# Causal attention and a PReLU MLP on one Trainium2 core: last outputs stored by half, first K loads on ACT's queue, four roundings of x moved to ACT, residues of sums of x spread over more steps

## The chip, the cores and the metric

The kernel runs on one core of a Trainium2 chip. The metric is the device time of one execution in microseconds (us), taken as the median of several executions. Five engines run their own instruction streams and wait for one another by semaphores: PE (TensorE, matrix products), DVE (VectorE), ACT (ScalarE), POOL (GpSimd) and SP (SyncE, which here only issues DMAs). DMAs go through queues that an engine's stream feeds; here nearly all are issued by SP.

## The reference

```python
scores = scale * q @ k.T            # per batch (4) and head (12): 448 x 448, D = 64
scores = where(causal mask, -1e9, scores) - max
attn = exp(scores); attn = attn / (sum(attn) + 1e-9)
a = attn @ v                         # (4, 12, 448, 64), fp32
x = a.transpose(0, 2, 1, 3).reshape(1792, 768)
h = x @ w_in                         # 768 -> 2048
g = max(h, 0) + alpha * min(h, 0)    # PReLU, alpha per column
out = g @ w_out                      # 2048 -> 768, fp32
```

## The kernel before

**Attention.** The 12 heads of a batch are 6 pairs of heads, so there are 24 pairs p in all; TURNS gives their order, batches 0 and 1 first (p 0 to 11), then 2 and 3 (p 12 to 23). They run as a software pipeline: iteration n of the loop in `attention` goes once through the list ORDER, and an entry such as `EX30+2` does step EX30 of pair p = n - 2. For one pair the steps are: load q and k (LQ, LK), scores on PE into PSUM (S0 to S2, SF), row maximum on DVE (MX, line 429), exponential with row sum on ACT (EX, line 444), reciprocals of the seven columns of row sums at once on DVE (RC, `row_rec`), scaling of the rows on POOL, or on DVE for a few (NO), transposes on PE (PT, line 472), their copies out of PSUM on ACT or DVE (C), and the product with v (AV, line 491). All engines but SP go through the same list, so the list sets the order of each engine's stream. AV has lag 4: iteration n does AV of pair n - 4.

**What AV leaves.** The result x of a pair (128x448 in PSUM) is rounded to fp32r as x_hi (XH on ACT for the parts named B, XN on DVE for those named N, which are the pairs 10, 11, 14, 15, 22, 23 by `part_of`), its rest x_lo is computed on DVE (XL, line 553) and stored to a DRAM scratch. The MLP's first product uses a Strassen-like scheme for all groups but the first, so sums T1 to T4 of parts of x are kept in fp32 in `spare` (XF, DVE), and each of the 16 sums must be rounded (`t_hi`) and its residue taken and stored (`t_lo`). In EARLY these are marked `T` (both on POOL); in FIRST they are `th` (rounding on ACT) and `tl` (residue on DVE, then its store when the next one is taken).

**The weights** arrive as 8-byte doubles and are decoded per piece of 128x384: abs on ACT (line 243), clamp on POOL (246), four operations on DVE (249 to 257), add on POOL (260). Then casts to fp32r on ACT (lines 287, 317) and the low parts on POOL (291, 320). The table EARLY says in which iteration of the attention which of these are done for the first group: `A` abs, `C` clamp, `D:i:k` k of the DVE operations of piece i, `+` add, `LD` load of the next piece, `cast:` and `sub:` the two halves of a split. LOADV says how many of the loads of v are issued in the iteration in which AV of pair p is done.

**The MLP.** The 2048 columns are 8 groups g of 256, each for two blocks of tokens bp; together 16 units q = 2g + bp. A unit has four result tiles X, Y, Z, W of h in PSUM; `h_act` applies PReLU on DVE, `g_hi` (line 731, ACT) and `g_lo` (line 735, POOL) split it, and `o_half` (line 769, PE) multiplies a 128-row tile with one half (384 columns) of w_out and adds it to `acc` (line 775 on ACT for group 0, line 777 on DVE after that). For the last group the finished rows go to the output (line 785, SP). Behind the attention, group 0 is written out by hand: FIRST lists for the steps 0 to 28 what the engines do beside PE; steps 1 to 10 have one `h_mms` of unit 1 each on PE, the later ones one or two `o_half`. Entries are `act.1X` (PReLU of unit 1's X), `gh`, `gl`, `D`, `abs`, `clamp`, `add`, `S` (a sum of weight pieces), `cast`, `sub`, `th`, `tl`.

**DMA counters.** The hardware queue's transfers report to eight counters in turn, shared by all engines that issue; an issue waits until the transfer that used its counter before, eight earlier in the program, has landed.

Of the kernel before, what the change touches and what calls it, by code (L numbers as in the profile page):

```python
# [10 lines left out]
F32 = mybir.dt.float32  # L11
# [5 lines left out]
ALU = mybir.AluOpType  # L17
# [16 lines left out]
LOADV = {0: 2, 1: 2, 2: 2, 3: 1, 9: 4, 10: 3, 12: 1, 13: 2, 14: 2, 15: 2}  # L34
TURNS = [(0, 0), (0, 1), (0, 2), (0, 5), (1, 0), (1, 1), (1, 3), (1, 4), (0, 3), (0, 4), (1, 2), (1, 5)]
ORDER = """
E2+4 LK+0 LQ+0 LT+4 NO00+3p NO10+3p MX11+2 NO21+3p NO11+3p EX10+2 EX11+2 MX20+2 NO20+3p MX21+2 EX20+2 NO30+3p MX00+2 EX00+2 AV+4 S2+2 LV+4 PT1+3 PT0+3 PT2+3 EX21+2 MX01+2 EX01+2 XF+4 XN+4 XH+4 C10+3a MX30+2 XL+4 EX30+2 ED+4 C00+3d C21+3d RC+2 NO01+2p C20+3a PT3+3 S0+1 S1+1 SF+1 C30+3a EA+4 MX10+1 ST+4
# [9 lines left out]
7: gl.1Y clamp.i2.1 S.S1.1 th
8: D.i2.1.2 tl cast.S1.1
9: D.i2.1.2 load sub.S1.1 abs.i3.1 cast.L1.1
10: add.i2.1 clamp.i3.1 sub.L1.1 th  # L50
11: act.1W act.1Z tl
12: D.i3.1.2 S.S2.1 cast.A22.1
13: D.i3.1.2 load sub.A22.1 th
14: add.i3.1 S.S3.1 cast.A11.1 tl
# [63 lines left out]
def kernel(  # L118
# [455 lines left out]
    def run(it, n=None):  # L574
# [4 lines left out]
        "LV": load_v_next, "RC": row_rec, "AV": av, "XH": x_hi, "XN": x_hi_plain, "XF": x_sums, "XL": x_lo, "ST": lambda p: flush(stores),  # L579
# [8 lines left out]
    for nm in "qk":  # L588
        steps["L" + nm.upper()] = lambda p, nm=nm: p and load(p, nm)
# [168 lines left out]
    def o_half(q, n, t, hf):  # L758
# [318 lines left out]
```

## Time and profile before

| quantity | value |
|---|---|
| time, 3 runs | 627.35, 628.26 (median), 629.2 us |
| the profiled execution's own time | 627.45 us |
| its span, first to last instruction | 625.7 us |
| PE busy | 608.4 us, 97% of the span, 3528 matmuls |
| DVE / ACT / POOL busy | 501.7 (80%) / 277.2 (44%) / 395.7 us (63%) |
| HBM read / written | 105.00 / 14.68 MB, 191 GB/s over the span |

The span covers the first to the last instruction; the execution's own time is 1.75 us longer than that. "Busy" counts computing instructions only. PE is busy nearly everywhere, so what is left is in the few places where PE has nothing to do: at the start, at stalls during the attention and just behind it, and at the end, where the last outputs are still under way. A stall of another engine costs only where PE ends up waiting for it.

### The profile page before, as it was taken

The page shows a single profiled execution, that of the slowest core. Times are in us where ns is not written, and L with a number is a line of the kernel's source. Part 1 is how long each engine was busy: PE and PEld are TensorE (multiplying, and loading weights), DVE is VectorE, ACT ScalarE, POOL GpSimd, SP SyncE. Part 2 cuts the span into 40 slices and gives each one's busy share as a digit, 9 for nine tenths or more (in the row PEclk, how much of TensorE's full clock was granted, in tenths as well). Part 3 has the DMA queues.
Part 4 walks back from the last instruction along what each step waited for, and adds up shares of the span by engine and source line. Part 5 has one row for each costly group of instructions (what it writes and reads, how often), then busy time and mean ns, then how long its engine had stood idle before and what let it go on. Part 6 is the DMA issues. An engine that isn't in the chain of part 4 may idle for free.

```text
span 625.7 us, 10851 instructions
## 1 busy us (share of the span) xinstructions
PE 608.4 (97%) x3528; PEld 529.6 (85%) x3528; DVE 501.7 (80%) x1117; ACT 277.2 (44%) x766; POOL 395.7 (63%) x530
## 2 busy tenths in 40 slices
PE   7899999999999899999999999999999999999996
PEld 3566676666878799899999999989999999999896
DVE  5699999999688579798689879868977987895363
ACT  5789897898344655231333323232332323232110
POOL 4455676868776758865775687567667766763120
PEclk9899999999999999999999999999999999999999
DMA  5874477642868468656765775786667567554535
GB/s 130 194 184 135 117 223 208 204 134 70 281 188 287 136 207 288 212 181 204 246 190 176 230 215 155 222 250 177 191 221 221 179 218 224 166 175 140 178 137 201
DMA packets 87736, 120.39 MB, mean 192 GB/s; under 512 B 12032, under 2 KB 64256, under 8 KB 87680
## 3 DMA queue, kind: packets, MB, share of 16 engines
q1 hardware_dynamic: 87520, 119.48, 62.6%
q8 instruction: 28, 0.46, 0.3%
q10 hardware_dynamic: 160, 0.23, 0.1%
q14 instruction: 28, 0.23, 0.1%
HBM read 105.00 MB, written 14.68 MB: 191 GB/s over the span
## 4 chain that ended last, share of the span: by engine, by line
PE 82%; DVE 6%; DMA 4%; SPq 3%; POOL 2%; ACT 1%; issue 1%; POOLq 0%; ACTq 0%; DVEq 0%
PE o L769 35%; PE heldY L676 11%; PE heldX L676 8%; PE heldZ L676 5%; PE pt L472 5%; PE a L491 4%; PE s L417 3%; PE h_V L676 3%; PE heldW L676 2%; DMA v<-in_v_dram 2%; PE s L409 2%; SPq L352 2%; ACT p L444 1%; SPq L355 1%; DVE s L429 1%
## 5 line engine op out<-in xcount | busy, mean ns | idle before, releaser
L777 DVE TENSOR_TENSOR acc<-o,acc 128x384 f32<-128x384 f32 x196 | 107.5, 552 | 71.2 <-PE o L769 70.9
L398 POOL TENSOR_SCALAR p<-p,rs 128x128 f32<-128x128 f32 (+3 forms) x164 | 80.4, 512 | 57.2 <-DVE rs L453 34.4
L444 ACT ACTIVATE p<-s,nm 128x256 f32<-128x256 f32 (+3 forms) x168 | 82.0, 497 | 20.1 <-DVE nm L429 19.8
L769 PE MATMUL o<-wo,g_X 128*128 128x384 f32 x336 | 76.8, 335 | 2.9 <-ACT g_X L731 1.8
L769 PE MATMUL o<-wo,g_Z 128*128 128x384 f32 x336 | 76.6, 335 | 1.1 <-DVE t_W L722 0.6
L429 DVE CUSTOM_DVE_ANT_0 s<-s,mask 128x256 f32<-128x256 f32 (+3 forms) x168 | 70.9, 480 | 8.0 <-PE s L417 5.7
L769 PE MATMUL o<-wo,g_W 128*128 128x384 f32 x336 | 76.6, 334 | 0.3 <-POOL g_W L735 0.3
L769 PE MATMUL o<-wo,g_Y 128*128 128x384 f32 x336 | 76.4, 335 | 0.0
L769 PEld LDWEIGHTS o<-wo,g_X 128*128 128x128 f32 x336 | 60.3, 188 | 6.7 <-ACT g_X L731 2.1
L769 PEld LDWEIGHTS o<-wo,g_Z 128*128 128x128 f32 x336 | 60.2, 188 | 4.9 <-DVE t_W L722 0.9
L769 PEld LDWEIGHTS o<-wo,g_W 128*128 128x128 f32 x336 | 59.9, 188 | 0.6 <-POOL g_W L735 0.6
L769 PEld LDWEIGHTS o<-wo,g_Y 128*128 128x128 f32 x336 | 60.0, 188 | 0.0
L491 PEld LDWEIGHTS a<-ptf,v 128*64 128x64 f32 x384 | 27.7, 136 | 35.1 <-issue 10.5
L472 PEld LDWEIGHTS pt<-ident,p 128*128 128x128 f32 x384 | 44.6, 144 | 13.7 <-issue 10.9
L491 PE MATMUL a<-ptf,v 128*64 128x64 f32 (+3 forms) x384 | 49.5, 387 | 3.6 <-DMA v<-in_v_dram 2.3
L472 PE MATMUL pt<-ident,p 128*128 128x128 f32 x384 | 48.7, 279 | 2.4 <-DVE p L460 1.3
L260 POOL TENSOR_TENSOR y_i<-y_i,x_i 128x384 f32<-128x384 f32 x32 | 33.5, 1048 | 27.1 <-DVE x_i L257 27.1
L260 POOL TENSOR_TENSOR y_o<-y_o,x_o 128x384 f32<-128x384 f32 x32 | 32.4, 1012 | 15.9 <-DVE x_o L257 15.9
L394 ACT ACTIVATE ptf<-pt 128x512 f32<-128x512 f32 (+1 forms) x72 | 38.3, 574 | 8.6 <-PE pt L472 8.6
L735 POOL TENSOR_TENSOR g_Z<-t_Z,g_Z 128x384 fp32r<-128x384 f32 (+1 forms) x16 | 20.0, 1247 | 31.1 <-ACT g_Z L731 31.1
L417 PE MATMUL s<-kr,qr 64*128 64x128 f32 (+2 forms) x288 | 38.4, 394 | 0.0
L243 ACT ACTIVATE x_i<-raw_i 128x384 f32<-128x384 f32 x32 | 17.8, 555 | 46.3 <-DMA raw_i<-in_moe_w_in_dram 46.3
(177 smaller groups left out, 1339.4 us busy)
## 6 DMA issues: line engine op xcount, KB each, us to landing
lo_T<-low_T SPq DMA_DIRECT2D x28, 512.0 KB, 4.6
lo_B<-low_B SPq DMA_DIRECT2D x25, 512.0 KB, 4.7
raw_i<-in_moe_w_in_dram SPq DMA_DIRECT2D x32, 384.0 KB, 3.8
raw_o<-in_moe_w_out_dram SPq DMA_DIRECT2D x32, 384.0 KB, 3.3
lo_T<-low_T SPq DMA_DIRECT2D x28, 384.0 KB, 3.9
lo_B<-low_B SPq DMA_DIRECT2D x25, 384.0 KB, 3.9
lo_N<-low_N SPq DMA_DIRECT2D x16, 512.0 KB, 4.8
lo_N<-low_N SPq DMA_DIRECT2D x16, 384.0 KB, 4.5
```

The costliest lines, as they stand in the source:

```text
L260: nc.gpsimd.tensor_tensor(out=y, in0=y, in1=xf, op=ALU.add)
L394: eng.activation(out, x, AF.Copy, scale=side)
L398: eng.tensor_scalar(out=out, in0=x, scalar1=side, scalar2=1.0, op0=ALU.mult, op1=ALU.mult)
L417: nc.tensor.matmul(ps[:, o : o + lim], T["q", p][half(j), i * QP : (i + 1) * QP], T["k", p][half(j), :lim], start=(o == 0), stop=(n > 0 or ...
L429: nc.vector.tensor_tensor_reduce(out=t, in0=t, in1=masks[1] if i == NQ else masks[0][:, (NQ - 1 - i) * QP :], scale=-SCALE, scalar=MOST_F3 ...
L444: nc.scalar.activation(T["p", p, i][:, j, : t.shape[1]], t, AF.Exp, scale=-1.0, bias=T.pop(("nm", p, i, j)), accum_out=T["sm", p][:, z : z ...
L472: nc.tensor.transpose(ps[:, j - js[0], c], t[:, j, c * QP : (c + 1) * QP], T["ident"])
L491: nc.tensor.matmul(out[half(j), c * QP :], vs[b % 2][:, hp, c, j], x[:, c * QP : S], start=(c == 0), stop=(c == NQ),)
L676: nc.tensor.matmul(ps, w[:, u, k * P : (k + 1) * P], x, start=(first and i == 0), stop=(i == len(mms) - 1), skip_group_check=True,)
L735: nc.gpsimd.tensor_tensor(out=l, in0=hts.pop((q, nm)), in1=h, op=ALU.subtract)
L769: nc.tensor.matmul(ps[:, :NH], x, w, start=(i == 0), stop=(i == 3 * GC - 1))
L777: nc.vector.tensor_tensor(out=a[:, cols], in0=ps[:, :NH], in1=a[:, cols], op=ALU.add)
```

## The change

1. **Outputs.** Each 128x384 half of the last group is stored as soon as it is added; before, both halves of a tile were stored together behind the second half, the very last tile apart. The output bytes are the same; SP issues 24 more DMAs.
2. **First K.** The K of pairs 0, 1 and 2 (six DMAs of 64x448) are issued by ACT at its start; before, only pair 0's were, and those of pairs 1 and 2 came from SP.
3. **RA.** For pair 0 alone the seven reciprocals are taken in two steps: six columns in a new step RA behind EX01, the seventh in RC as before. In the list ORDER, `RA+2` stands between `EX01+2` and `XF+4`, so ahead of `MX30+2`.
4. **ROUND.** x_hi of the pairs 10, 11, 14, 15 is rounded by ACT (XH), not DVE (XN).
5. **EARLY and LOADV.** The decoding of the first group's weights and the sums T are given to other iterations (before: DVE operations in iterations 12 to 19 numbered 2, 2, 2, 2, 2, 1, 1, 1; now 1, 1, 3, 3, 1, 0, 3, 1), and v of batches 2 and 3 is loaded in 2, 3, 2 DMAs with pairs 12 to 14, not 1, 2, 2, 2 with 12 to 15.
6. **FIRST.** The residues (`th`, `tl`) run from step 2 to 24, not 2 to 16; `gh.1X`, `gl.1X` stand at step 16, one step earlier, and `1W` at 17, with the casts S2 and S3 one step later.

```diff
-    5: "A:0", 6: "C:0 D:0:1", 7: "D:0:2 A:1", 8: "C:1", 12: "D:0:1 LD D:1:1 T",
-    13: "+:0 D:1:2 A:2 cast:A21", 14: "C:2 D:1:1 LD D:2:1 +:1", 15: "D:2:2 A:3 T",
-    16: "C:3 sub:A21 D:2:1 LD D:3:1 cast:A22", 17: "D:3:1 T", 18: "+:2 D:3:1 sub:A22 cast:L1", 19: "D:3:1 LD T",
-    20: "+:3 cast:A11", 21: "sub:L1 cast:A12", 22: "sub:A11 cast:L0 A:4", 23: "sub:A12 C:4 A:5", 24: "sub:L0 C:5",
-    25: "LD +:4 T D:5:4 LD", 26: "C:6 C:7 D:6:4 LD T T +:6 T T",
+    5: "A:0", 6: "C:0 D:0:1", 7: "D:0:2 A:1", 8: "C:1", 12: "D:0:1 LD T", 13: "+:0 D:1:1 A:2 cast:A21",
+    14: "C:2 D:1:3 LD", 15: "D:2:3 +:1", 16: "D:2:1 LD T A:3 cast:A22", 17: "+:2 C:3 cast:L1 cast:A11",
+    18: "D:3:3 T", 19: "D:3:1 LD +:3 sub:A21", 20: "T sub:A22 cast:A12", 21: "sub:L1 sub:A11 cast:L0",
+    22: "sub:A12 sub:L0 A:4", 23: "C:4 A:5", 24: "C:5", 25: "LD +:4 T D:5:4 LD", 26: "C:6 C:7 D:6:4 LD T T +:6 T T",
 }
 FRONT = {25: "D:4:4", 26: "+:5 A:6 A:7"}
...
-LOADV = {0: 2, 1: 2, 2: 2, 3: 1, 9: 4, 10: 3, 12: 1, 13: 2, 14: 2, 15: 2}
+LOADV = {0: 2, 1: 2, 2: 2, 3: 1, 9: 4, 10: 3, 12: 2, 13: 3, 14: 2}
+ROUND = (10, 11, 14, 15)
 TURNS = [(0, 0), (0, 1), (0, 2), (0, 5), (1, 0), (1, 1), (1, 3), (1, 4), (0, 3), (0, 4), (1, 2), (1, 5)]
...
-15: cast.S2.1 sub.A11.1 th
-16: cast.S3.1 sub.S2.1 S.S4.1 tl
-17: gh.1X gl.1X sub.S3.1 abs.o0.1 st
-18: gh.1W gl.1W cast.A12.1 clamp.o0.1
+16: gh.1X gl.1X cast.S2.1
+17: gh.1W gl.1W cast.S3.1 sub.S2.1 S.S4.1
+18: th sub.S3.1 abs.o0.1 cast.A12.1
+19: tl clamp.o0.1 sub.A12.1
...
     def load_first():
         load(0, "q")
-        load(0, "k", nc.scalar)
+        for p in range(3):
+            load(p, "k", nc.scalar)
...
-    def row_rec(p):
+    def row_rec(p, cols=slice(0, 2 * NQ + 1)):
         sm = T["sm", p]
-        r = T["r", p] = ap["b2"].tile([P, 2 * NQ + 1], F32, tag="rs", name=f"rs_{p}")
-        nc.vector.tensor_tensor(out=sm, in0=sm, in1=least, op=ALU.add)
-        nc.vector.reciprocal(r, T.pop(("sm", p)))
+        if ("r", p) not in T:
+            T["r", p] = ap["b2"].tile([P, 2 * NQ + 1], F32, tag="rs", name=f"rs_{p}")
+        nc.vector.tensor_tensor(out=sm[:, cols], in0=sm[:, cols], in1=least[:, cols], op=ALU.add)
+        nc.vector.reciprocal(T["r", p][:, cols], sm[:, cols])
+
+    def row_rec_some(p):
+        if p == 0:
+            row_rec(p, slice(0, 2 * NQ))
+
+    def row_rec_rest(p):
+        row_rec(p, slice(2 * NQ if p == 0 else 0, 2 * NQ + 1))
...
     def x_hi_plain(p):
         h, nm, k = part_of(p)
-        if nm[0] == "N":
+        if nm[0] == "N" and p not in ROUND:
             copy(hi_of(h, nm, k), T["a", p], nc.vector)
 
     def x_hi(p):
         h, nm, k = part_of(p)
-        if nm[0] != "N":
+        if nm[0] != "N" or p in ROUND:
...
-        steps["L" + nm.upper()] = lambda p, nm=nm: p and load(p, nm)
+        steps["L" + nm.upper()] = lambda p, nm=nm: p > (2 if nm == "k" else 0) and load(p, nm)
...
-            if (bp, n, t) == (NBP - 1, 1, blocks[bp][1] // P - 1):
-                wide = [cols]
-            else:
-                wide = [slice(0, DM)] if hf == 1 else []
-            for cs in wide:
-                for part, rows in out_rows(bp, n, t):
-                    nc.sync.dma_start(out=out[rows, cs], in_=a[part, cs])
+            for part, rows in out_rows(bp, n, t):
+                nc.sync.dma_start(out=out[rows, cols], in_=a[part, cols])
```

PE's own stream is the same before and after. The tables move the other engines' instructions as follows.

On ACT at the start of the program, before, the stream goes from two loads of pair 0's K (`kr_0`) to the table load for the exponential, two small copies that make the masks, and the first exponential (`L444`) of pair 0:

```order
L352 DMA kr_0_116<-in_k_dram 64x448 x2
L931 ACT_TABLE_LOAD
L931 ACTIVATE mask384_146<-mk_151 128x128 [waits Pool_49]
L934 ACTIVATE mask448_147<-mk_151 64x64 x2
L444 ACTIVATE p_0_1_216,sm_0_217<-s_0_0_0_185,nm_0_1_0_197 128x256 [waits DVE_49]
```

With the change (the lines are some four further down the file) the same place reads:

```order
L352 DMA kr_0_116<-in_k_dram 64x448 x2
L352 DMA kr_1_119<-in_k_dram 64x448 x2
L352 DMA kr_2_122<-in_k_dram 64x448 [waits DMAHW1_49]
L352 DMA kr_2_122<-in_k_dram 64x448 [waits DMAHW4_49]
L935 ACT_TABLE_LOAD
L935 ACTIVATE mask384_152<-mk_157 128x128 [waits Pool_49]
L938 ACTIVATE mask448_153<-mk_157 64x64 x2
L445 ACTIVATE p_0_1_216,sm_0_217<-s_0_0_0_188,nm_0_1_0_200 128x256 [waits DVE_49]
```

Four more DMA issues stand ahead of the table load, and two of them wait for a transfer's counter: DMAHW1 is that of the first half of pair 0's K, DMAHW4 that of the first of the two small loads `qd` of pair 0 by SP.

On DVE in pair 0 of the attention, before, the last row maximum (`L429` with mask448, the step MX30) stands ahead of the sums' correction and the reciprocal (`L452`, `L453`), after which pair 1 begins (`s_1_...`) and one scaling of pair 0 follows (`L460`):

```order
L429 ISA s_0_0_1_186,nm_0_0_1_231<-s_0_0_1_186,mask384_146 128x128
L429 ISA nm_0_0_1_231 128x1
L429 ISA s_0_2_195,nm_0_3_0_234<-s_0_2_195,mask448_147 128x448
L429 ISA nm_0_3_0_234 128x1
L452 TENSOR_TENSOR sm_0_217<-sm_0_217,least_61 128x7
L453 RECIPROCAL rs_0_237<-sm_0_217 128x7
L429 ISA s_1_0_0_241,nm_1_1_0_251<-s_1_0_0_241,mask384_146 128x256
L429 ISA nm_1_1_0_251 128x1
L460 TENSOR_SCALAR p_0_1_216<-p_0_1_216,rs_0_237 128x256
```

Now six of the seven columns are taken ahead of that row maximum:

```order
L430 ISA s_0_0_1_189,nm_0_0_1_231<-s_0_0_1_189,mask384_152 128x128
L430 ISA nm_0_0_1_231 128x1
L454 TENSOR_TENSOR sm_0_217<-sm_0_217,least_61 128x6
L455 RECIPROCAL rs_0_234<-sm_0_217 128x6
L430 ISA s_0_2_198,nm_0_3_0_237<-s_0_2_198,mask448_153 128x448
L430 ISA nm_0_3_0_237 128x1
L454 TENSOR_TENSOR sm_0_217<-sm_0_217,least_61 128x1
L455 RECIPROCAL rs_0_234<-sm_0_217 128x1
L430 ISA s_1_0_0_243,nm_1_1_0_253<-s_1_0_0_243,mask384_152 128x256
L430 ISA nm_1_1_0_253 128x1
L469 TENSOR_SCALAR p_0_1_216<-p_0_1_216,rs_0_234 128x256
```

So MX30 of pair 0, and pair 1's maxima behind it, now stand behind a reciprocal that needs the sixth exponential of pair 0 (step EX01), and the scaling at `L460` still stands behind pair 1's first maximum.

On ACT behind the attention, where group 0's second unit begins its output products (`acc_...` are copies of finished tiles out of PSUM, `wi_...` casts of weights, `g_1_X` the rounding of unit 1's X, `xw<-acc1` the rounding of a sum of x), before:

```order
L775 ACTIVATE acc_0_0_2801<-o_0_0_0_1_3022 128x384
L287 ACTIVATE wi_1_A11_3030<-y_i2_0_2919 128x256
L775 ACTIVATE acc_0_1_2802<-o_0_0_1_1_3036 128x384
L287 ACTIVATE wi_1_S2_3044<-S2_1_3006 128x256
L394 ACTIVATE xw_63<-acc1_65 128x448
L775 ACTIVATE acc_0_2_2803<-o_0_0_2_1_3048 128x384
L287 ACTIVATE wi_1_S3_3056<-y_i3_0_2814 128x256
L775 ACTIVATE acc_1_0_2804<-o_0_1_0_0_3063 128x384
L731 ACTIVATE g_1_X_3071<-t_1_X_2902 128x512
```

and now:

```order
L784 ACTIVATE acc_0_0_2803<-o_0_0_0_1_3014 128x384
L287 ACTIVATE wi_1_A11_3026<-y_i2_0_2918 128x256
L784 ACTIVATE acc_0_1_2804<-o_0_0_1_1_3029 128x384
L784 ACTIVATE acc_0_2_2805<-o_0_0_2_1_3041 128x384
L740 ACTIVATE g_1_X_3049<-t_1_X_2902 128x512
L287 ACTIVATE wi_1_S2_3052<-S2_1_3000 128x256
L784 ACTIVATE acc_1_0_2806<-o_0_1_0_0_3054 128x384
L740 ACTIVATE g_1_W_3062<-t_1_W_2983 128x512
L287 ACTIVATE wi_1_S3_3065<-y_i3_0_2816 128x256
```

`g_1_X` moved up past the casts S2 and S3, the rounding of a sum of x and the copy `acc_1_0`, and is followed at one copy's distance by `g_1_W`; the cast S3 went behind both.

## Rows read from the trace of the kernel before

**Rows 1.** Busy time by engine, us 220 to 620: us, then PE, PEld, DVE, ACT, POOL.

```profile
220.00:620.00 400.00, 399.72 (x2149) 379.19 (x2147) 318.07 (x537) 118.99 (x268) 250.50 (x278) 1.00 0.64 200
```

**Rows 2.** Chain of waits, PE's: waited for, us in total, times, longest.

```profile
PE a L491 <- DMA v<-in_v_dram: 2.3, 3, 1.2
PE o L769 <- ACT g_X L731: 1.8, 1, 1.8
...
PE o L769 <- POOL g_X L735: 1.1, 1, 1.1
...
PE o L769 <- DVE t_W L722: 0.6, 1, 0.6
PE o L769 <- ACT acc L775: 0.5, 1, 0.5
```

**Rows 3.** Timeline, the last addition: start, us, engine, line, operation, [idle before <-releaser].

```profile
620.36 0.56 DVE L777 TENSOR_TENSOR acc<-o,acc 128x384 f32<-128x384 f32 x1 [0.49 <-PE o L769]
```

**Rows 4.** DMA issues of 612.5 to 613.2 and 620.9 to 625.7: KB, us to landing.

```profile
out_dram<-acc SPq DMA_DIRECT2D x1, 192.0 KB, 1.9
...
out_dram<-acc SPq DMA_DIRECT2D x1, 192.0 KB, 3.9
```

**Rows 5.** Timeline of ACT behind the attention.

```profile
205.60 0.42 ACT L287 ACTIVATE wi_S<-S 128x256 fp32r<-128x256 f32 x1 [2.72 <-DVE S L265]
...
208.16 0.42 ACT L287 ACTIVATE wi_S<-y_i 128x256 fp32r<-128x256 f32 x1 [1.29 <-DVE y_i L265]
```

**Rows 6.** Timeline of POOL at the same place.

```profile
209.75 1.44 POOL L735 TENSOR_TENSOR g_X<-t_X,g_X 128x512 fp32r<-128x512 f32 x1
```

**Rows 7.** Busy time by engine: one light iteration; the sum of the seven that follow.

```profile
63.89:69.97 6.08, 6.08 (x49) 4.08 (x47) 5.76 (x22) 5.47 (x18) 3.38 (x8) 1.00 0.38 113
...
sum 45.43, PE 44.92 PEld 31.61 DVE 42.81 ACT 38.29 POOL 34.07; mean PE 6.42 PEld 4.52 DVE 6.12 ACT 5.47 POOL 4.87
```

**Rows 8.** Groups by line, DVE and ACT, us 70 to 150: busy, mean ns of one.

```profile
L396 DVE CAST xp<-a 128x448 fp32r<-128x448 f32 x4 | 2.5, 618 | 0.0
...
L394 ACT ACTIVATE xw<-a 128x448 fp32r<-128x448 f32 x7 | 3.8, 547 | 0.1
```

**Rows 9.** Timeline of PE, first AV of batch 3.

```profile
124.08 0.34 PE L491 MATMUL a<-ptf,v 128*64 128x64 f32 x4 [0.77 <-DMA v<-in_v_dram]
```

**Rows 10.** Timeline of the start: issues by ACT's and SP's queue, ACT, DVE.

```profile
0.74 1.20 ACTq L352 DMA_DIRECT2D kr<-in_k_dram  x2
...
1.96 1.28 ACT L931 ACT_TABLE_LOAD   x1 [1.96 <-issue]
...
6.28 0.43 DVE L429 CUSTOM_DVE_ANT_0 s<-s,mask 128x256 f32<-128x256 f32 x1 [4.72 <-PE s L417]
...
6.80 0.47 ACT L444 ACTIVATE p<-s,nm 128x256 f32<-128x256 f32 x1 [2.83 <-DVE nm L429]
...
11.21 3.89 SPq L376 DMA_DIRECT2D v<-in_v_dram  x7
```

**Rows 11.** DMA issues of us 0 to 2.2 and 2.2 to 3.5.

```profile
kr<-in_k_dram ACTq DMA_DIRECT2D x2, 112.0 KB, 3.0
...
qd<-in_q_dram SPq DMA_DIRECT2D x2, 16.0 KB, 2.7
```

**Rows 12.** Timeline of PE, first 32 us.

```profile
11.81 0.41 PE L472 MATMUL pt<-ident,p 128*128 128x128 f32 x2 [1.26 <-DVE p L460]
...
17.34 1.51 PE L491 MATMUL a<-ptf,v 128*64 128x448 f32 x8 [0.66 <-ACT ptf L394]
...
20.94 0.34 PE L491 MATMUL a<-ptf,v 128*64 128x64 f32 x4 [0.39 <-DMA v<-in_v_dram]
...
22.26 3.38 PE L472 MATMUL pt<-ident,p 128*128 128x128 f32 x16
...
29.81 1.91 PE L472 MATMUL pt<-ident,p 128*128 128x128 f32 x16
```

**Rows 13.** Granted TensorE clock, us 22 to 25: the number behind POOL's column.

```profile
22.00:25.00 3.00, 3.00 (x14) 2.74 (x13) 1.60 (x4) 2.12 (x5) 0.00 (x0) 0.50 0.40 116
```

More of the change, by code (lines that the diff above doesn't have):

```diff
@@ L33 @@
 REAR = {26: "D:7:4 LD +:7"}
-LOADV = {0: 2, 1: 2, 2: 2, 3: 1, 9: 4, 10: 3, 12: 1, 13: 2, 14: 2, 15: 2}
+LOADV = {0: 2, 1: 2, 2: 2, 3: 1, 9: 4, 10: 3, 12: 2, 13: 3, 14: 2}
+ROUND = (10, 11, 14, 15)
 TURNS = [(0, 0), (0, 1), (0, 2), (0, 5), (1, 0), (1, 1), (1, 3), (1, 4), (0, 3), (0, 4), (1, 2), (1, 5)]
 ORDER = """
-E2+4 LK+0 LQ+0 LT+4 NO00+3p NO10+3p MX11+2 NO21+3p NO11+3p EX10+2 EX11+2 MX20+2 NO20+3p MX21+2 EX20+2 NO30+3p MX00+2 EX00+2 AV+4 S2+2 LV+4 PT1+3 PT0+3 PT2+3 EX21+2 MX01+2 EX01+2 XF+4 XN+4 XH+4 C10+3a MX30+2 XL+4 EX30+2 ED+4 C00+3d C21+3d RC+2 NO01+2p C20+3a PT3+3 S0+1 S1+1 SF+1 C30+3a EA+4 MX10+1 ST+4
+E2+4 LK+0 LQ+0 LT+4 NO00+3p NO10+3p MX11+2 NO21+3p NO11+3p EX10+2 EX11+2 MX20+2 NO20+3p MX21+2 EX20+2 NO30+3p MX00+2 EX00+2 AV+4 S2+2 LV+4 PT1+3 PT0+3 PT2+3 EX21+2 MX01+2 EX01+2 RA+2 XF+4 XN+4 XH+4 C10+3a MX30+2 XL+4 EX30+2 ED+4 C00+3d C21+3d RC+2 NO01+2p C20+3a PT3+3 S0+1 S1+1 SF+1 C30+3a EA+4 MX10+1 ST+4
 """
@@ L42 @@
 2: gh.0Z gl.0Z D.i0.1.2 load abs.i1.1 clamp.i1.1 sub.o2.0 th
-3: D.i1.1.2 add.i0.1 sub.o3.0 tl th
-4: D.i1.1.2 load tl
-5: act.1Y act.1X add.i1.1 th
+3: D.i1.1.2 add.i0.1 sub.o3.0 tl
+4: D.i1.1.2 load th
+5: act.1Y act.1X add.i1.1
 6: gh.1Y tl abs.i2.1
[L47 to L54, printed above, removed]
-15: cast.S2.1 sub.A11.1 th
-16: cast.S3.1 sub.S2.1 S.S4.1 tl
-17: gh.1X gl.1X sub.S3.1 abs.o0.1 st
-18: gh.1W gl.1W cast.A12.1 clamp.o0.1
-19: D.o0.1.1 sub.A12.1
-20: D.o0.1.1
+7: gl.1Y clamp.i2.1 S.S1.1
+8: D.i2.1.2 cast.S1.1 th
+9: D.i2.1.2 load sub.S1.1 cast.L1.1
+10: add.i2.1 sub.L1.1 tl abs.i3.1
+11: act.1W act.1Z clamp.i3.1
+12: S.S2.1 cast.A22.1
+13: D.i3.1.2 sub.A22.1 th
+14: D.i3.1.2 load S.S3.1 cast.A11.1
+15: add.i3.1 sub.A11.1 tl
+16: gh.1X gl.1X cast.S2.1
+17: gh.1W gl.1W cast.S3.1 sub.S2.1 S.S4.1
+18: th sub.S3.1 abs.o0.1 cast.A12.1
+19: tl clamp.o0.1 sub.A12.1
+20: D.o0.1.2 th
 21: D.o0.1.2 load
-22: add.o0.1
+22: add.o0.1 tl th
 23: gh.1Z gl.1Z abs.o1.1
-24: clamp.o1.1
-25: D.o1.1.1
+24: clamp.o1.1 tl
+25: D.o1.1.1 st
 26: D.o1.1.1
@@ L578 @@
     steps = {
-        "LV": load_v_next, "RC": row_rec, "AV": av, "XH": x_hi, "XN": x_hi_plain, "XF": x_sums, "XL": x_lo, "ST": lambda p: flush(stores),
+        "LV": load_v_next, "RA": row_rec_some, "RC": row_rec_rest, "AV": av, "XH": x_hi, "XN": x_hi_plain, "XF": x_sums, "XL": x_lo, "ST": lambda p: flush(stores),
     }
```

## The prediction

> **What bounds the kernel now.** I read the page first: PE is busy 97% of the span, the other engines 44 to 80%. The sum is therefore made of the places where PE has nothing to do, and each part of the change is asked what it does to one of them. Second, the busy time by engine from 220 to 620 us: PE 399.72 of 400 us at full granted clock [rows 1]. PE's stream is the same after the change, so that stretch takes as long as before: a us gained ahead of it arrives at the end whole, and nothing is to be had inside it. Third, PE's waits [rows 2]: 1.8 and 1.1 us for unit 1's X (ACT, then POOL), 0.6 for PReLU's W, 0.5 for a copy on ACT, all four in group 0's output products just behind the attention, and 2.3 us for v. Fourth, the two ends: the last addition ends at 620.92 us [rows 3], the last output lands some 4 us later [rows 4]; and in the first 22 us PE waits for pair 0's exponentials and for v [rows 12]. Fifth, the attention in its steady state by iterations: a light one takes 6.08 us, PE busy all of it; the seven that follow take 45.43 [rows 7].
>
> **The end.** The last 128x384 write, 192 KB, takes 3.9 us to land; a write of the same size, at 612.6, when the engines had nothing else, took 1.9 [rows 4]. The difference is the backlog: unit 15's tiles are finished first in all their left halves and then in all their right ones, and each was written whole behind the right half, so all its bytes left in the second half of its time. By half, the bytes leave at half that rate. I take 1.9 for the last write: **−2.0** (0 to −2.1). The 24 more issues cost SP about 0.6 us each (1.20 for two in [rows 10]), 14 us over the last two units, in which SP has nothing else to issue; if that cover were missing, the last issue would be late by what is left of it.
>
> The Trainium skill speaks against this part: "DMA: Bandwidth & Descriptors", section "Measured (HBM→SBUF, 128 partitions, SWDGE, issued from GpSimd)", asks for DMAs of 1 MiB or more and says that transfers under 64 KB are mostly descriptor cost. By it, halving 384 KB writes would buy nothing, and the end term would be 0. The trace shows a 192 KB write at either time, so it is the queue ahead of it that decides here; the rule's case is rival C.
>
> **Behind the attention.** The four stalls sum to 1.8 + 1.1 + 0.6 + 0.5 = 4.0 us [rows 2]. X's rounding on ACT stood behind two casts that wait 2.72 us for the sum S2 and 1.29 us for another sum, both from DVE [rows 5]; POOL's half of it, 1.44 us, began only at 209.75 [rows 6]. Now it stands ahead of both casts, and DVE has lost three of the residues that lay ahead of those sums (each 448 columns; the nearest row is the 618 ns of [rows 8]). That ended at 209.75 + 1.44 = 211.2, and PE had stood 1.8 + 1.1 = 2.9 us for X by then, so X costs nothing if it is done by 208.3. Freed of 2.72 + 1.29 it can be, at about 208. I take **−3.2**: the X stalls nearly gone, 0.3 left, and half of 0.6 + 0.5. Bounds −4.0, when all four go, and −1.5, when X waits for PReLU on DVE instead and only one of its two stalls goes. The spread residues themselves cost ACT and DVE as much as before, in later steps where DVE has room; if that cover is gone, W is late next, by 0.6 each.
>
> **The attention.** Seven light iterations would be 7 × 6.08 = 42.56 us; the excess is 45.43 − 42.56 = 2.87. DVE is busy 42.81 of it [rows 7], more than the room of 42.56, and since every engine follows the list, DVE sets the pace. Three of the four roundings that go to ACT lie there: 3 × 0.618 = 1.85 us [rows 8] off DVE, which leaves 40.96. ACT gains 3 × 0.547 = 1.64 and one cast from a later iteration, 0.42 [rows 5]: 38.29 + 2.1 = 40.4, still under 42.56 on average. But iterations 16 and 17 now hold an abs and a cast, or two casts, beside ACT's 5.47 of a light one: 5.47 + 0.9 = 6.4, over 6.08 by about 0.3 each, as is 13 (before too). So I leave 1.2 of the excess standing: **−1.7** (−0.5 to −2.9). The moved decode operations (13 before, 13 now) cost nothing in sum.
>
> **v of batch 3.** Its first product waits 0.77 us for v [rows 9]. The seven loads now end one iteration, some 6 us, sooner, well beyond the wait: **−0.9**, with a little for the weight loads behind the product that waits (−0.8 to −1.0).
>
> **The front.** ACT's two K issues begin at 0.74 and land 3.0 us later; SP's small `qd` loads, issued from 2.25 on, take 2.7 [rows 10, 11]. ACT's sixth issue waits for the first of them: about 2.2 + 2.7 = 5.0. Then 0.6 for the issue, 1.28 for the table [rows 10]: 6.9, and behind it stands the mask copy, for which DVE's first maximum waits. That maximum came 0.52 us ahead of the first exponential (6.28 to 6.80, [rows 10]); with about 0.4 for the copy the first exponential comes at 7.9, 1.1 us late. Then RA: MX30 of pair 0 now waits for the sixth exponential, and EX30, the last column's reciprocal and the scaling that the first transposes need come behind it one after the other (448 columns at about 0.65, twice, estimated from 0.43 to 0.47 for 256): some 1.3 us more. So the first transposes go from 11.81 to about 14.2, and the first AV opens at 19.6 instead of 17.34 [rows 12]. That is no loss by itself: in the end this AV waits for v, until 20.94 [rows 12]. SP has four K issues less ahead of v, 4 × 0.6 = 2.4 us, of which I take 1.8, since v's issues also wait for counters: v lands at about 19.1. The AV takes 8 + 4 + 4 products, about 1.9 us: it ends at 21.5 instead of 21.28 (20.94 + 0.34), 0.2 late.
>
> Against that stands the granted clock. From 22 to 25 us it was 0.50, the lower of the two levels, 1.2 GHz [rows 13], after the pieces of PE work between 12 and 21 us with gaps. The 16 transposes in that stretch took 3.38 us; the same 16 next time 1.91 [rows 12]: 1.47 lost. Now the wait is longer and lies earlier (PE has little from about 10.5 to 14.2), so the low stretch probably falls into it, where PE's work isn't what is waited for, and the first AV finds the full clock: gain 1.2 net of the 0.2, and I take **−1.0** (−1.5 to +1.7; at the worst the low stretch falls on the full work once more and the late AV costs 0.2 beside 1.47).
>
> The Trainium skill, "TensorE: Matmul & The Clock Gate", section "HAM oscillation — how this bites in real kernels", says that idle gaps between bursts of matmuls send the clock to its lower level, each time anew. By it, a longer pause in the front could cost another stretch at half clock: the front would lose about 1.5 us and not gain 1.0; that is rival D.
>
> **The sum** against the profiled execution's own time of 627.45: −2.0 − 3.2 − 1.7 − 0.9 − 1.0 = −8.8, so 618.65. That execution lies 0.81 below the median of 628.26, so on the scale of the median **619.5 us**.
>
> **Rivals.**
> A, the forecast as worked out: 0.49.
> B, other engines keep their waits: ACT sets the pace in the attention (−0.5), X is late by PReLU (−1.5), the front is even (0); with −2.0 and −0.9 that is −4.9, 623.4 us. For it speak ACT's 6.4 us in iterations 16 and 17 and the 0.3 that X has left: 0.20.
> C, halving pays nothing, the write at the end takes 3.9 as before: 619.5 + 2.0 = 621.5. Against it is the 1.9 of a lone write of that size: 0.10.
> D, the lower clock falls on work twice: +1.7 for −1.0 in the front, 622.2 us: 0.12.
> E, the other side: ACT is held at its fifth or sixth issue well beyond 5.0. Every exponential stands behind it, and each us there delays all of PE's work by one once v is in. Slower begins when 8.8 + 1.9 = 10.7 us are lost so, that is with ACT held until 15.7. Against it: no load in the first 3.5 us took over 3.0 to land [rows 11]. 0.03.
> F, the change doesn't do what it says: the stalls taken away come back as others of the same length, and the end is as before: 628. Against it is that the stretch from 220 on has no wait in which gains could go [rows 1]: 0.06.
>
> **The numbers.** About 0.3%, 1.9 us, is what this measurement can tell from no change. A to D are all faster by more: 0.91. F is the same: 0.06; E slower: 0.03. The range goes from the sum of all best bounds (−2.1 − 4.0 − 2.9 − 1.0 − 1.5 = −11.5, 616.8, and 0.8 for the spread of the runs) at 616.0 to rival B with nothing gained behind the attention (624.9) at 625.0. Left out are E and F and a tail of B and D, in all under 0.2.
>
> **What would show it.** First exponential near 7.9 and first transposes near 14.2; the granted clock at 0.5 before the first AV and not behind it; 16 transposes near 1.9 us at about 22 us. Seven iterations of the attention in under 44 us with DVE near 41. No wait for v in the first AV of batch 3. PE's waits for X under 0.5 us. The last 192 KB landing in about 1.9 us, and still no wait from about 212 us on. The prediction is wrong if PE waits for ACT in iterations 16 to 18, if the granted clock falls behind the first AV again, or if the last output lands as late after the last addition as before.

## The result and the profile after

The change made the kernel slower: 633.86 us (631.51 to 636.16, 6 runs) against 628.39 of the kernel before in the same comparison, ratio 1.0083, 95% interval 1.0057 to 1.0109. The profiled execution took 634.32 us, its span 632.5, 6.8 us more than before. PE's stream is the same, so its steps can be laid beside one another. Starts of AV(n), the AV of iteration n, and of other steps, by PE's timeline in both profiles:

| stretch | before | after | difference | forecast |
|---|---|---|---|---|
| start to AV(5) | 27.07 | 26.07 | −1.0 | −1.0 |
| AV(5) to AV(12) | 42.90 | 43.29 | +0.4 | 0 |
| AV(12) to AV(22), ten iterations | 64.65 | 74.71 | **+10.1** | −2.6 (attention, v) |
| AV(22) to the first output product | 58.73 | 58.75 | 0.0 | 0 |
| that to group 1's first product | 25.98 | 23.75 | −2.2 | −3.2 |
| that to the end of the last addition | 401.59 | 403.07 | +1.5 | 0 |
| that to the end of the span | 4.78 | 2.86 | −1.9 | −2.0 |

PE's waits in the changed kernel, in the form of [rows 2]:

```profile
PE s L418 <- ACT ptf L395: 6.9, 2, 4.9
PE pt L481 <- DVE p L469: 3.0, 1, 3.0
...
PE o L778 <- POOL g_X L744: 1.5, 1, 1.5
PE heldX L685 <- DMA lo_B<-low_B: 1.2, 1, 1.2
PE o L778 <- DVE t_W L731: 0.7, 1, 0.7
...
PE a L500 <- DMA v<-in_v_dram: 0.5, 1, 0.5
```

The 6.9 us for `ptf`, the copies of the transposes by ACT, are new; so is the wait for `lo_B`, a reload of a low part of x. ACT itself was waiting, as its timeline shows, and behind it DVE for a DMA (the waits of DVE, then the timelines of SP's queue, DVE, ACT and PE at the first of the two places):

```profile
DVE acc L397 <- DMA low_T<-acc: 8.7, 2, 5.8
```

```profile
106.34 0.53 SPq L516 DMA_DIRECT2D low_T<-acc  x1
106.91 2.77 SPq L377 DMA_DIRECT2D v<-in_v_dram  x3
...
110.89 0.62 DVE L397 COPY acc<-a 128x448 f32<-128x448 f32 x1 [5.85 <-DMA low_T<-acc]
...
111.54 0.54 ACT L395 ACTIVATE xw<-a 128x448 fp32r<-128x448 f32 x1 [5.35 <-DVE acc L397]
...
112.63 2.92 PE L418 MATMUL s<-kr,qr 64*128 64x256 f32 x10 [4.94 <-ACT ptf L395]
```

In iteration 17 DVE wants to copy x of pair 13 into `acc` (the profile's name for the buffer in which the sums of x are kept; step XF, line 556), and can't until a store from that same place has landed. Everything else waits behind it. Then PE pays a second time, by its clock (busy time by engine, granted clock behind POOL's column):

```profile
107.00:112.00 5.00, 0.69 (x3) 0.29 (x2) 1.11 (x3) 0.46 (x2) 0.77 (x2) 0.87 0.64 179
112.00:116.00 4.00, 3.37 (x12) 1.98 (x14) 3.68 (x14) 4.00 (x15) 1.96 (x5) 0.50 0.40 127
120.00:124.00 4.00, 4.00 (x32) 3.04 (x32) 3.90 (x15) 2.55 (x8) 0.86 (x3) 1.00 0.45 143
```

PE was busy 0.69 of 5 us; the clock fell to 0.50, the 1.2 GHz level, and the ten score products that came next took 2.92 us, where the twelve at 18.49 us (a row further down), nearly all at full clock, took 1.58. The Trainium skill, "TensorE: Matmul & The Clock Gate", section "HAM oscillation — how this bites in real kernels", has idle gaps between bursts followed by the lower clock; this row agrees. Iteration 17 took 13.43 us instead of 6.86, iteration 21 8.73 instead of 6.08:

```profile
102.05:115.48 13.43, 8.49 (x46) 5.65 (x46) 7.27 (x29) 7.41 (x27) 6.26 (x13) 0.82 0.61 177
```

The store's source is tile k = 1 of the sum T1 of the first half of the batches. These lines, which the change does not touch, say why the two meet: T1 and T3 have the same slots for both halves h, T2 and T4 do not.

```python
n = {"T1": 0, "T3": 2, "T2": 8 if h else 4, "T4": 10 if h else 6}[nm] + k
return spare[:, n * S : (n + 1) * S]
```

`T` in EARLY takes the next residue on POOL, in place; its store leaves with LT of the next iteration; and pair 13 overwrites the slot in iteration 17. Before, that `T` stood in iteration 15, its store left in 16; the change put it into 16. The fourth `T`, moved from 19 to 20, meets pair 17 in iteration 21 in the same way.

The other ends, in the forms of [rows 10, 12, 13]: the start, with its granted clock from 16 to 18 us,

```profile
6.16 1.28 ACT L935 ACT_TABLE_LOAD   x1 [6.16 <-DMA qd<-in_q_dram]
...
8.32 0.47 ACT L445 ACTIVATE p<-s,nm 128x256 f32<-128x256 f32 x1
...
14.80 3.75 PE L481 MATMUL pt<-ident,p 128*128 128x128 f32 x16 [2.99 <-DVE p L469]
18.49 1.58 PE L418 MATMUL s<-kr,qr 64*128 64x256 f32 x12
19.99 1.95 PE L500 MATMUL a<-ptf,v 128*64 128x448 f32 x16
...
22.73 1.91 PE L481 MATMUL pt<-ident,p 128*128 128x128 f32 x16
```

```profile
16.00:18.00 2.00, 2.00 (x11) 2.00 (x11) 1.92 (x10) 1.91 (x9) 0.00 (x0) 0.50 1.20 201
```

and the last addition and the last write, to lay beside [rows 3, 4]:

```profile
629.08 0.56 DVE L786 TENSOR_TENSOR acc<-o,acc 128x384 f32<-128x384 f32 x1 [0.49 <-PE o L778]
```

```profile
out_dram<-acc SPq DMA_DIRECT2D x1, 192.0 KB, 2.0
```

### The profile page after: what moved, and what is told of

Same layout as the page of the kernel before. It is cut to its first block, busy times and chain, and to the rows that moved or that the text cites. A ratio compares the mean times of both kernels' runs of the same rounds, so it can differ in the third digit from the quotient of the medians.

```text
span 632.5 us, 10875 instructions
## 1 busy us (share of the span) xinstructions
PE 611.5 (97%) x3528; PEld 531.8 (84%) x3528; DVE 500.5 (79%) x1115; ACT 278.6 (44%) x770; POOL 395.3 (62%) x530
## 4 chain that ended last, share of the span: by engine, by line
PE 58%; DMA 1%; DVE 1%; issue 0%; POOLq 0%; POOL 0%; ACT 0%; SPq 0%; ACTq 0%
PE o L778 31%; PE heldY L685 10%; PE heldX L685 7%; PE heldZ L685 5%; PE heldW L685 2%; PE h_V L685 2%; DMA lo_B<-low_B 1%; POOLq L1076 0%; POOL g_Z L744 0%; DVE y_i L253 0%; DVE acc L786 0%; DVE t_Z L731 0%; ACT g_Z L740 0%; DVE t_Z L728 0%; DVE t_Y L731 0%
## 5 line engine op out<-in xcount | busy, mean ns | idle before, releaser
L500 PE MATMUL a<-ptf,v 128*64 128x448 f32 (+3 forms) x384 | 49.3, 392 | 1.2 <-DMA v<-in_v_dram 0.5
L418 PE MATMUL s<-kr,qr 64*128 64x384 f32 (+2 forms) x288 | 42.1, 404 | 7.6 <-ACT ptf L395 6.9
```

Source lines behind the costliest of these rows:

```text
L418: nc.tensor.matmul(ps[:, o : o + lim], T["q", p][half(j), i * QP : (i + 1) * QP], T["k", p][half(j), :lim], start=(o == 0), stop=(n > 0 or ...
L500: nc.tensor.matmul(out[half(j), c * QP :], vs[b % 2][:, hp, c, j], x[:, c * QP : S], start=(c == 0), stop=(c == NQ),)
```

## The experiments

The kernel before took 630.3 to 630.5 us beside these runs, 2 us more than above, so ratios are compared. "Ten iterations" is AV(12) to AV(22) of the run's profile, 64.65 us in the kernel before and 74.71 in the changed one.

### Is it the store that is waited for?

**t_back**: two of the sums moved back, all else as changed.

```diff
-    14: "C:2 D:1:3 LD", 15: "D:2:3 +:1", 16: "D:2:1 LD T A:3 cast:A22", 17: "+:2 C:3 cast:L1 cast:A11",
-    18: "D:3:3 T", 19: "D:3:1 LD +:3 sub:A21", 20: "T sub:A22 cast:A12", 21: "sub:L1 sub:A11 cast:L0",
+    14: "C:2 D:1:3 LD", 15: "D:2:3 +:1 T", 16: "D:2:1 LD A:3 cast:A22", 17: "+:2 C:3 cast:L1 cast:A11",
+    18: "D:3:3 T", 19: "D:3:1 LD +:3 sub:A21 T", 20: "sub:A22 cast:A12", 21: "sub:L1 sub:A11 cast:L0",
```

> The changed kernel, with the second and the fourth of the early sums T given to iterations 15 and 19 instead of 16 and 20, so that the store of each residue leaves SP one iteration before DVE copies the next x into the same part of the spare tile. Theory W (the copy waits for that store to land, 5.85 us in iteration 17 and a second one three to four iterations later): both stalls go, some 6.6 and 2.6 us of PE's time, and the kernel takes 624.6 us, 1.0% under before. Rival R (ACT's extra roundings and casts hold the copies of the transposes, the store is only what the profile names): PE's two waits for ACT's copies stay within 1 us of 6.9 and the time stays over 631. Rival L (three loads of v in one iteration crowd the queue): no more than 2 us are won, 632.

Measured: 627.42 us, ratio 0.9947 (0.9923 to 0.9970); ten iterations 67.58 us; no wait of DVE for a store is left. Theory W holds against R and L, but only 7.1 of the 9.2 us came: iterations 15 and 20 now take 8.21 and 8.14 us, since POOL's `T` stands where POOL and DVE are already full: the `T` of iteration 19 runs at the start of 20, where PE then waits 1.5 us for POOL's scaling of p, and in 15 DVE's decode operations are stretched (last section). PE's wait of 1.5 us at the end of 15 has no releaser in the profile, so that it comes from there is argued.

**slot12**: no instruction moves, but the colliding tile has a buffer of its own.

```diff
+        if (h, nm, k) == (1, "T1", 1):
+            n = 12
```

> The changed kernel, where the second half of T1 of batches 2 and 3 goes to an unused slot of the spare tile and not over that of batches 0 and 1, whose residue's store was waited for; no instruction moves. Theory W (a write that has to wait for the store of what it overwrites): the first stall, 5.85 us of DVE, goes and with it about 6.5 us of PE's time, the second stays: 627.5 us on a chip where the kernel before takes 628.4, ratio 0.998. Rival R (ACT's or DVE's load in iterations 16 and 17): PE's wait of 4.9 us for ACT's copy stays, ratio over 1.006.

Measured: 628.69 us, ratio 0.9970 (0.9948 to 0.9992), where 0.998 was expected. Ten iterations 68.69 us. DVE's waits for stores:

```profile
DVE acc L399 <- DMA low_T<-acc: 2.5, 1, 2.5
```

The 5.85 us wait is gone, and with it PE's wait of 4.9 us for ACT's copy (1.6 us, behind the second store, are left); rival R falls. This is the cleanest of the runs: the order of every engine is that of the changed kernel, and one slot number is worth 6.0 us of the ten iterations and 1.1% of the time.

**loadv_old**: the loads of v as before, in the changed kernel.

```diff
-LOADV = {0: 2, 1: 2, 2: 2, 3: 1, 9: 4, 10: 3, 12: 2, 13: 3, 14: 2}
+LOADV = {0: 2, 1: 2, 2: 2, 3: 1, 9: 4, 10: 3, 12: 1, 13: 2, 14: 2, 15: 2}
```

> The changed kernel with the loads of v of batches 2 and 3 as before (1, 2, 2, 2 with pairs 12 to 15). Theory W: the store ahead of the first stall lands in 2.2 us instead of 4.4, since one load of v stands behind it, not three, but the copy still waits for it, some 3.6 us; the second stall stays at 2.6, and the first product of batch 3 waits for v again or the stall hides it: 632 us. Rival L: the crowd of loads is the cause, both stalls shrink under 1 us, 625. Rival R: no change, 634.

Measured: 635.29 us, ratio 1.0077 (1.0048 to 1.0107); ten iterations 73.41.

```profile
DVE acc L397 <- DMA low_T<-acc: 8.1, 2, 5.2
```

The wait is 5.2 us instead of 5.8, so the third load of v behind the store adds 0.6; rival L falls. My 3.6 falls as well: two loads of v stand behind the store, not one, and it took 3.8 us to land, not 2.2 (4.4 in the changed kernel).

**early_alone**: the lines of EARLY of the change's diff, and nothing else, in the kernel before.

> The kernel before with the table of the early work alone as in the changed kernel. Theory W: both stalls of DVE for the residues' stores appear in full, 4 to 6 us and 2 to 3 us, and the time is 635 us. Rival R (ACT's roundings, which are not in this kernel, make the stall): no wait of DVE for a store over 1 us, 628 or less. Rival L: v is loaded as before here, so no stall over 1 us, 628.

Measured: 640.51 us, ratio 1.0153 (1.0125 to 1.0182); ten iterations 74.28.

```profile
DVE acc L395 <- DMA low_T<-acc: 7.7, 2, 5.4
```

Without the four roundings on ACT the stall is the same, so R falls. It took 3 us more than expected (635 to 628.4 is 1.0105). The profile shows more than that: the ten iterations are 9.6 us longer than before, where I had expected 6.6 in all, and behind PE's waits for X the clock falls to 0.50, so that the stretch from the first output product to group 1 takes 28.58 us instead of 25.98.

### What the other parts are worth

The base is now **early_old**, the changed kernel with the same lines of EARLY turned back.

> The changed kernel with the whole table of the early work as before; everything else of the change stays. Theory W with the other terms as the changed kernel's profile shows them (end 1.9, behind the attention 2.2, batch 3's v 1.0, front 0.5 on the mean of the profiles, a new wait for a low part of 0.5 back): no wait for a store, and with nothing from the four roundings 1.9 + 2.2 + 1.0 + 0.5 - 0.5 = 5.1 us under the kernel before, ratio 0.992. If the roundings also relieve DVE as I had predicted, up to 1.8 more, ratio 0.989. Rival R (the change costs elsewhere in the attention, too): ratio 0.997 or more.

Measured: 625.74 us, ratio 0.9937 (0.9914 to 0.9960), between the two; ten iterations 65.93, 1.3 us over the kernel before although the wait for v of batch 3 is gone. Something else in the attention costs. All else of the change is still in, so the new EARLY alone makes the difference from 1.0083 to 0.9937; t_back, which moves only two `T` back and leaves the decode operations where the change put them, is within 0.1 points of it (0.9947).

**early_old_noround**:

```diff
-ROUND = (10, 11, 14, 15)
+ROUND = ()
```

> early_old with the four roundings back on DVE. Theory P (DVE sets the pace, the roundings were worth 1.7 us): 1.2 to 1.8 us slower than early_old. Theory X (x_lo on DVE now waits 0.3 to 0.6 us for ACT's rounding, which stands behind the exponentials, so that nothing is won): within 0.6 us of early_old.

Measured: 624.58 us, ratio 0.9916 (0.9889 to 0.9943); ten iterations 63.56. By the medians 1.2 us faster without the moved roundings, which the intervals don't separate; in the profiles 2.4 us. DVE's waits in early_old:

```profile
DVE low_N L563 <- ACT xp L396: 2.4, 4, 0.6
```

Four roundings, four waits, 2.4 us, none of which are in early_old_noround. The first seven of the ten iterations, in the form of [rows 7], early_old's and then early_old_noround's:

```profile
sum 46.30, PE 45.51 PEld 32.77 DVE 40.98 ACT 39.17 POOL 33.65; mean PE 6.50 PEld 4.68 DVE 5.85 ACT 5.60 POOL 4.81
```

```profile
sum 45.33, PE 44.92 PEld 31.72 DVE 42.58 ACT 38.27 POOL 33.92; mean PE 6.42 PEld 4.53 DVE 6.08 ACT 5.47 POOL 4.85
```

The move takes 1.6 us off DVE, near the 1.85 forecast, and the seven iterations get 1.0 us longer, not shorter. Theory P falls. Theory X had the wait right and its price wrong: in these iterations the move isn't worth nothing, it costs.

**round_xl_late**: early_old with XL moved in the list ORDER.

```diff
-MX30+2 XL+4 EX30+2 ED+4 C00+3d C21+3d RC+2
+MX30+2 EX30+2 ED+4 C00+3d C21+3d XL+4 RC+2
```

> early_old (roundings on ACT), with the step that takes x_lo on DVE moved behind DVE's decode operations and its copies of the transposes, ahead of the reciprocals. Theory X1 (the loss is DVE standing 0.6 us for ACT's rounding with its copies queued behind it): the waits for xp go and the attention is 1.2 to 1.8 us shorter than early_old's, as with the roundings on DVE. Rival X2 (the loss is on ACT: its own copies come 0.55 us later behind the rounding): under 0.5 us won.

Measured: 624.75 us, ratio 0.9917 (0.9893 to 0.9941); ten iterations 65.08. The four waits are gone, and 0.9 of the 2.4 us came back. So X1 and X2 both have a part; the rest I can't assign: ACT's own chain, 0.55 us longer, or XL's new place.

**early_old_front**: K of pairs 1 and 2 from SP, and no step RA (RC takes all seven columns).

```diff
-        for p in range(3):
-            load(p, "k", nc.scalar)
+        load(0, "k", nc.scalar)
```

> early_old with the start as before: K of pairs 1 and 2 from SP and all seven reciprocals of pair 0 at once. Theory C (the low clock falls on the first AV and the transposes behind it again, some 22 to 25 us; the first AV waits for v): 0 to 1.0 us slower than early_old, 0.5 on the mean. Rival D (the later exponentials and the low clock from 15 to 19 us cost as much as they give): within 0.3, or faster by up to 1.

Measured: 626.70 us, ratio 0.9953 (0.9929 to 0.9978), 1.0 us over early_old, not separated by the intervals. Its profiled execution is its slowest (631.42), with 4.5 us of waits for v. AV(5) started at 26.0 to 27.3 us in the profiles with the new front, at 27.1, 27.2 and here 25.4 with the old one. The low clock that theory C expects at 22 to 25 us isn't there: with the old start this execution has full clock and transposes of 1.91 us, to lay beside [rows 12, 13]:

```profile
22.00:25.00 3.00, 3.00 (x29) 2.58 (x27) 2.43 (x8) 2.55 (x6) 0.26 (x1) 1.00 0.42 112
```

```profile
22.01 1.91 PE L480 MATMUL pt<-ident,p 128*128 128x128 f32 x16
...
25.35 1.95 PE L499 MATMUL a<-ptf,v 128*64 128x448 f32 x16
```

So theory C's reason falls, at least for this execution, and what the new front is worth stays open: by the medians up to 1 us won, by the starts of AV(5) between 2.0 us lost and 1.1 won.

**early_old_wide**: the store of the last outputs (the last piece of the change's diff) turned back.

> early_old with the last outputs stored in whole rows as before. Theory Q (a queue of bytes ahead of the last write decides): last write 3.9 us again instead of about 2, time 1.9 us over early_old, ratio to the kernel before 0.3 points higher. Rival S (size of a write decides): within 0.3 us.

Measured: 627.45 us, ratio 0.9961 (0.9944 to 0.9979), 1.7 us over early_old by the medians (the intervals just overlap). Its last write beside early_old's:

```profile
out_dram<-acc SPq DMA_DIRECT2D x1, 192.0 KB, 3.9
```

```profile
out_dram<-acc SPq DMA_DIRECT2D x2, 192.0 KB, 1.9
```

Q holds: the same 192 KB land in 3.9 us behind whole rows and in 1.9 behind halves.

### What becomes of the gain behind the attention

**first_old**: the lines of FIRST turned back to those of before, in the changed kernel.

> The changed kernel with the step table behind the attention as before. Theory: that table gave some 2.2 us behind the attention and took 1.2 back in one wait for a reload of x's low part near 255 us; so with the old table the waits for X and W of 4 us return, the wait near 255 us goes, and the time is 1 us longer, 634.9. Rival: the wait near 255 us comes from elsewhere (the loads are crowded because of the halved outputs or the K loads) and stays: 636. The stalls in iterations 17 and 21 are not touched in either case.

Measured: 637.26 us, ratio 1.0124 (1.0092 to 1.0157). The wait near 255 us went and the waits for X (1.8 and 1.1) came back, as expected; that 2.6 us were lost and not 1.0 has a reason that I had not counted, the clock: behind the waits for X it falls to 0.50, and the stretch from the first output product to group 1 takes 27.36 us, 1.4 more than in the kernel before with the same waits. The next run shows it, too.

**noround_first_old**: the same on early_old_noround.

> early_old_noround with the step table behind the attention as before. Theory G (what the new table gains behind the attention, about 2.2 us, is given back within 50 us at waits for reloaded low parts, 2.4 us in the profile of early_old_noround): the waits for X and the copy return, those for low parts near 235 to 250 us go or shrink under 0.5, and the time is within 0.6 us of early_old_noround. Rival (the gain is kept): 1.7 to 2.2 us slower.

Measured: 626.50 us, ratio 0.9938 (0.9914 to 0.9961), 1.9 us over early_old_noround by the medians, 1.0 by the spans. The waits in early_old_noround that this run hasn't:

```profile
PE heldX L686 <- DMA lo_B<-low_B: 1.6, 1, 1.6
...
PE h_V L686 <- DMA lo_T<-low_T: 0.6, 1, 0.6
```

And what this run has instead, PE's timeline and the granted clock of the two stretches behind it:

```profile
208.62 0.62 PE L779 MATMUL o<-wo,g_X 128*128 128x384 f32 x2 [1.79 <-ACT g_X L741]
210.34 0.44 PE L779 MATMUL o<-wo,g_X 128*128 128x384 f32 x1 [1.09 <-POOL g_X L745]
```

```profile
210.48:212.48 2.00, 2.00 (x9) 2.00 (x10) 0.00 (x0) 2.00 (x7) 2.00 (x3) 0.72 0.03 10
212.48:214.48 2.00, 2.00 (x8) 2.00 (x8) 1.68 (x3) 1.09 (x3) 0.92 (x2) 0.50 0.00 0
```

So the new table saves the waits for X and, in these profiles, 1.5 us of half clock behind them (27.51 us from the first output product to group 1, 25.98 in the kernel before), and gives 1.6 + 0.6 + 0.2 = 2.4 back where PE now arrives before its reloads. Of the 3.8 us that the new table saves ahead of group 1 in these two profiles, 1.0 to 1.4 are left at the end; the medians say 1.9, as the rival has it, and the intervals overlap. So G's mechanism, a loss at the reloads, is seen, but its number (within 0.6 us) falls: part of the gain is kept, and how much isn't settled.

**load_later**: one weight load of the second unit issued two steps later, on early_old_noround.

```diff
-9: act.2Y D.i1.1.2 load cast.o3.0 sub.o2.0
+9: act.2Y D.i1.1.2 cast.o3.0 sub.o2.0
-11: act.2Z abs.i2.1 clamp.i2.1
+11: act.2Z load abs.i2.1 clamp.i2.1
```

> early_old_noround with the fourth weight load of the second unit's steps issued at step 11 instead of 9, so that the reload of a low part stands ahead of it on SP's queue. Theory B (SP stands at that weight load until DVE frees its buffer, and four reloads of low parts then leave in one burst and take 6 to 8 us each): the wait for the first low part, 1.6 us, goes, and the kernel is 1 to 2 us faster than early_old_noround. Rival (the transfers are limited by the bytes on the way, not by SP's stand): the wait moves to the next low part, within 0.5 us.

Measured: 623.56 us, ratio 0.9890 (0.9866 to 0.9914), 1.0 us under early_old_noround by the medians (the intervals overlap); the wait for `lo_B` is gone, those for two `lo_T` (0.6 and 0.3) stay. By its median it is the best version: 1.1% under the kernel before, 1.9 points under the change as made.

## Why the prediction was wrong

1. **The step that failed** is "The moved decode operations (13 before, 13 now) cost nothing in sum". It counted DVE's operations and passed over the `T` entries that the same table moves. Their work costs the same in any iteration, but each ends in a store, and a later pair overwrites what is stored. Two of them went past the last iteration in which the store lands in time. By slot12 (the first wait alone) and t_back (both) this is worth 1.1% and 1.4% of the time, about as much as all forecast gains together (8.8 us). The decode operations themselves cost little: t_back keeps their new places. Without the step's fault the change would still have won under half of the forecast, some 4 us (early_old, 0.9937). No rival had it: I read what is waited for in the trace of before, and there this wait was zero. It was not far from showing: the store of T1's second tile had landed 3.0 us ahead of the copy (101.89 and 104.88 us in that trace), against 6 to 7 us of one iteration by which the change moves it.
2. **The attention term, −1.7**, failed by itself as well. "DVE sets the pace" was read from 42.81 busy us in a room of 42.56. DVE's busy time did fall as forecast, to 40.98 us against the forecast 40.96 (early_old), but the seven iterations took 46.30 us, so DVE's busy time doesn't set the pace. On DVE the roundings waited for nothing; on ACT they stand behind six exponentials, and DVE's x_lo waits for each, some 0.6 us. Measured: +2.4 us over the ten iterations of the profiles, about +1.2 by the medians, not separated. What does make the seven longer than 42.56 stays open: round_xl_late takes the four waits away and gets back 0.9 of the 2.4. Rival B had the direction (ACT as the pace) and not the size.
3. **The end, −2.0**: −1.9, and early_old_wide shows its cause. What decides is how many bytes still stand ahead of the last write, not its size, which is the same in both; rival C falls. The rule of the Trainium skill, "DMA: Bandwidth & Descriptors", section "Measured (HBM→SBUF, 128 partitions, SWDGE, issued from GpSimd)", by which the prediction had the halves buy nothing, is not borne out for these last stores (3.9 us behind whole rows, 1.9 behind halves); the page's figures are for loads into SBUF.
4. **v of batch 3, −0.9**: the wait of 0.77 is gone in the changed kernel, and in early_old, where no stall of DVE could hide it; right.
5. **Behind the attention, −3.2**: −2.2. ACT's half of X came in time; POOL's did not. It stood behind a decode addition, which itself waited 2.22 us for DVE's decode, and a low part, and I had not moved them out of its way:

```profile
214.80 1.13 POOL L260 TENSOR_TENSOR y_i<-y_i,x_i 128x384 f32<-128x384 f32 x1 [2.22 <-DVE x_i L257]
215.89 1.12 POOL L291 TENSOR_TENSOR wi_A<-y_i,wi_A 128x256 fp32r<-128x256 f32 x1
216.98 1.44 POOL L744 TENSOR_TENSOR g_X<-t_X,g_X 128x512 fp32r<-128x512 f32 x1
```

And "the stretch from 220 on takes as long as before" did not hold: it took 1.5 us longer, of which 1.2 are the wait for the reload `lo_B`. I read it as a slack: PE's full busy time there hid how late the reloads came, and what PE gained ahead of them it lost at the first that came late. That is argued: early_alone, which gained nothing there, has a wait of 1.0 us for `lo_B` too, and load_later, which only moves a weight load on SP's queue, takes that wait away.
6. **The front, −1.0**: in the changed kernel's profile all came as written (exponentials at 8.32 for 7.9, transposes at 14.80 for 14.2, the half clock in the pause and on the first transposes, full behind them, transposes of 1.91 us at 22.7), and the size is 1.0. But the term rests on the low clock from 22 to 25 us in the trace of before, and early_old_front, with the old start, has full clock there. So that the number was met is luck in part; it depends on which execution is laid beside which. The line "no load in the first 3.5 us took over 3.0 to land", which spoke against rival E, was misread as well: pair 0's q took 3.2 us. ACT was held until 6.16, so E stayed out even so.

## What to carry to other kernels

Before moving a step to a later iteration, list what it writes, who stores or reads it, and which later step reuses that buffer; the distance of that reuse is a due date which a trace without the wait doesn't show, though the landing time of the store and the start of the overwriting step do. A table that fits (the same operations, better spread) must be checked for such dates entry by entry. Work moved from a busy engine to a less busy one helps only if the new engine reaches it as early; here its place behind six exponentials made the relieved engine wait. And an engine that is 100% busy over a long stretch doesn't show how closely its transfers arrive ahead of it: a gain in front of such a stretch can be lost in part inside it, as here.

## What the runs showed of the hardware that was not expected

A decode operation of DVE stretches when it starts while one of POOL's two-input operations (TENSOR_TENSOR) is running. In t_back the same form of decode operation took 0.55 us at one place and 1.38 us at another, where POOL was at the `T` of the same iteration (two operations of DVE, then two of POOL):

```profile
86.06 0.55 DVE L253 SCALAR_TENSOR_TENSOR y_i<-raw_i,x_i 128x384 int32<-128x384 int32 x1
...
94.08 1.38 DVE L253 SCALAR_TENSOR_TENSOR y_i<-raw_i,x_i 128x384 int32<-128x384 int32 x1
```

```profile
93.28 0.55 POOL L399 TENSOR_SCALAR xw<-acc 128x448 fp32r<-128x448 f32 x1
93.91 1.14 POOL L578 TENSOR_TENSOR acc<-acc,xw 128x448 fp32r<-128x448 f32 x1
```

The longer one ends 0.41 us after POOL's 1.14 us operation. Two more in t_back started under such an operation of POOL; they took 1.25 and 1.20 us and ended 0.42 us after it, so most of the added time looks like waiting for its end. One that started ahead of POOL's operation (at 199.90 us) took 0.56. The Trainium skill, "SBUF — State Buffer", section "SBUF: two separate sides", describes a pair of ports that the two engines lock for whole instructions; the rows fit that. A table that spreads DVE's work should therefore look at what POOL does in the same iteration. Second, the clock: the same two waits for X of 1.8 and 1.1 us left the clock at full speed in the profiled execution of the kernel before and cost 1.5 us of half clock in that of noround_first_old, so a stall's price can be more than its length. It need not be the kernel that makes the difference: beside these runs the kernel before took 631.5 to 635.1 us in its executions with a mean granted clock of 0.985 to 0.988, and 627.2 to 630.6 in those with 0.994 to 0.997. A single profile therefore doesn't settle a microsecond that hangs on the clock.
